# A transformer block's feed-forward stage: two of the seven gate/up products in a stage of their own ahead of the passes, with a second level of seven

## The chip, the core and the metric

The kernel runs on one core of a Trainium2 chip. TensorE (PE) multiplies, VectorE (DVE) and ScalarE (ACT) read its results out of PSUM and prepare operands, GpSimd (POOL) helps with operands in SBUF, and SyncE (SP) issues every DMA, in order. The metric is the device time of one execution in microseconds.

## What is computed

One block of a transformer on 2048 tokens of width 1024, in float32: a modulated layer norm, an attention with a memory over four segments of 512 tokens, a residual, a second modulated layer norm, and a gated feed-forward part with F = 3584 hidden columns:

```
h = layernorm(x) * (1 + ca) + sa
x = x + ga * attention(h)                       # 4 segments of 512 tokens, 32 heads
h = layernorm(x) * (1 + cb) + sb                # h2_d in the kernel, stored transposed: [D, T]
x = x + gb * ((gelu(h @ w_gate) * (h @ w_up)) @ w_down)
```

The change lies in `h @ w_gate` and `h @ w_up`.

## The kernel before

Stages, in the order of TensorE's work: attention; the output projection (`projections`, line 805 on, matmuls of L763), four segments in blocks `block(s, nb)` of 4 tiles; the gate/up stage (`gate_up`, L1188); the down projection (`down`, L1402).

Every float32 product is made of three matmuls of the faster type fp32r: each operand is cut into a high part (ACT, a copy) and a low part (DVE or POOL, the difference), and hi·hi, hi·lo and lo·hi are added up in PSUM. This is what `cut` does (L902 and L904). A matmul here has 128 x 128 weights and 512 columns.

The gate/up stage goes over the tokens in two passes of 1024, and in each pass over the 28 chunks of 128 hidden columns (the second pass backwards): 56 steps, called chunks below, m = 0 to 55. For one chunk, tokens and width are halved, and gate and up are the two column halves. So there are 2 x 2 blocks on each side, a11 to a22 of h2 and b11 = upper gate, b12 = upper up, b21 = lower gate, b22 = lower up, and the four result blocks come from seven products instead of eight (the Winograd form of Strassen's method). Their numbers are those of the code: 1 = a11 b11, 2 = a12 b21, and 3 to 7 are products of sums. The results are gate of the first tokens = 1 + 2; up of the first tokens = 1 + 6 + 5 + 3; gate of the other tokens = 1 + 6 + 7 + 4; up of the other tokens = 1 + 6 + 7 + 5. A product is 4 x 3 = 12 matmuls, so a chunk has 84 and the stage 4704.

The order within a chunk is 1, 6, 2, 7, 5, 4, 3, in three PSUM banks: `pa` takes 1 and then 2 on top of it, `pb` takes 6, then 7 and then 4 on top, `pc` takes 5 and then 3. DVE reads a bank between two products that share it: `u2 = pb + c1` (L1203) after 6, `u3 = pb + c1` (L1213) after 7, `u3 = pc + u3` (L1217) after 5, `g2 = pb + c1` (L1221) after 4, `u2 = pc + u2` (L1226) after 3; then two multiplications in SBUF, `g1 * u2` (L1227) and `g2 * u3` (L1228). ACT copies product 1 to `c1` (L1199) and takes two gelus.

The order on PE, DVE, ACT, POOL and SP is the order in which the program is written. The work beside the products comes from generators in the list `sides`: `step()` is called at fixed places of a product and lets each generator go on by one piece. In the first pass `b_part` loads the weights of a chunk two ahead, forms the sums of `seven` (POOL, L908), cuts them into the tiles B (a ring of 8) and stores all seven to `bc_d`; the second pass reads them back (`b_ahead`). `a_part` and `a_next` make the operands A of h2 for a pass. `w_all` prepares w_down in the second pass (tiles T), and `norm_tiles` makes h2.

Of the kernel before, what the change touches and what calls it, by code (L numbers as in the profile page):

```python
# [36 lines left out]
def block_kernel(ctx: ExitStack, tc: tile.TileContext, x, c, wmod, wq, wkv, wo, beta, wg, wu, wd, out):  # L37
# [11 lines left out]
    mix_d = dram.tile([4 * L, L], F32, name="mix_d")  # L49

    bc_d = dram.tile([FC * 7 * P, 1024], F32, name="bc_d")
# [196 lines left out]
    def norm_tiles(src, dst, segs, jscale, jshift, name, tiles=range(4), wait=0, get=raw_tile, more=[]):  # L248
# [12 lines left out]
        def turn(q, h):  # L261
# [14 lines left out]
            send_h = lambda: nc.sync.dma_start(dv[:, 4 * h:4 * h + 4, tok:tok + P], hh.rearrange("p (k t) -> p k t", t=P))  # L276
# [11 lines left out]
    def norm_steps(toks, xs, load, turn, name, wait):  # L288
        if wait:
            for q in range(len(toks)):  # L290
                load(q)
                for _ in range(wait):
                    yield
                t, nm = xs[q], f"{name}{toks[q]}"
                mv, rs = norm_stats([t[:, :L], t[:, L:]], nm)
                for _ in range(3):
                    yield
                norm_scale([t], mv, rs, nm)
                for _ in range(wait - 2):
                    yield  # L300
                for h in range(2):
                    turn(q, h)
                    yield
            return
        for at in range(5 * len(toks) + 8):
            for q in range(len(toks)):
                k = at - 5 * q
                if k == 0:
                    load(q)
                elif k == 5:  # L310
                    t, nm = xs[q], f"{name}{toks[q]}"
                    st = norm_stats([t[:, :L], t[:, L:]], nm)
                elif k == 7:
                    norm_scale([t], *st, nm)
                elif k in (10, 11):
                    turn(q, k - 10)
            yield
# [409 lines left out]
    xrs = []  # L727
    waiting = [True]

    def x_tile(name):  # L730

        if xrs[0] is None:
            return raw_tile(name)[:, :L]
        xrs[1] += 1
        return f32(xrs[0][:, xrs[1] // 2 % 2, xrs[1] % 2 * L:(xrs[1] % 2 + 1) * L])
# [7 lines left out]
    def project(s, todo):  # L743
# [7 lines left out]
        for n, (i, nb) in enumerate(todo):  # L751
# [16 lines left out]
            store = lambda tok=tok, fs=fs, xr=xr: nc.sync.dma_start(x1_d[tok:tok + P, fs], xr)  # L768
# [43 lines left out]
    def projections():  # L812
# [5 lines left out]
        xrs.extend([wsp_tile("xr"), -1])  # L818
# [17 lines left out]
        sides.append(cols(3))  # L836
        yield from block(2, 0)
        sides.append([ff["b"](0), 2, "b"])
        second = ff["a"]((5, 4))
        operands = ff["a"]((1, 6, 2, 7), second)  # L840
        sides.append([chain(iter([None] * 10), islice(operands, 1)), 1, "n"])
        yield from block(3, 0)
        flush("bn")
        pw_close()
        xrs[0] = None
        ff["pools"](1)
        sides.append([chain(operands, second), 2, "a"])
        yield from block(2, 1)
        pev_close()
        ff["pools"](2)  # L850
        ff["release"]()
        sides.append([chain(iter([None] * 9), islice(ff["b1"], 1)), 1, "a"])
        yield from block(3, 1)

# [3 lines left out]
    PASSES = ((0, 1024), (1024, 1024))  # L858
    NCH = len(PASSES) * FC
# [3 lines left out]
    PRODUCTS = (1, 6, 2, 7, 5, 4, 3)  # L863
# [3 lines left out]
    def feed_forward():  # L867
# [8 lines left out]
        def a_place(i, kt, q):  # L876
            n = 0 if i == 1 else 1 if i in (6, 2) or (i == 7 and kt < 2) else 2 if i in (7, 5) or (i == 4 and kt < 2) else 3
            return ffp[n], f"A{i}_{kt}_{q}"

        def a_tile(i, kt, q, name):  # L880
            at, tag = a_place(i, kt, q)
            return at.tile([P, HM], F32R, name=name, tag=tag, bufs=1)
# [10 lines left out]
        A, B, X, done, loaded, held = {}, {}, {}, set(), [], []  # L893
        ops, raws, cutted = {}, {}, set()

        def parts(n, eng):

            w = 256 if eng is nc.gpsimd else L
            return [slice(k, min(k + w, n)) for k in range(0, n, w)]

        def cut(hi, lo, src, eng):
            nc.scalar.activation(hi, src, AF.Copy)  # L902
            for k in parts(src.shape[-1], eng):
                eng.tensor_sub(lo[:, k], src[:, k], f32(hi)[:, k])  # L904

        def diff(dst, a, b):
            for k in parts(L, nc.gpsimd):
                nc.gpsimd.tensor_sub(dst[:, k], a[:, k], b[:, k])  # L908

        def total(dst, a, b):  # L910
            for k in parts(L, nc.gpsimd):
                nc.gpsimd.tensor_add(dst[:, k], a[:, k], b[:, k])

        def put_a(p, i, kt, src, eng):
            hl = [a_tile(i, kt, q, f"A{p}_{i}_{kt}_{q}") for q in range(2)]
            cut(hl[0], hl[1], src, eng)
            A[p, i, kt] = hl

        def mix_rows(i):
            k = MIX.index(i)  # L920
            return mix_d[k * L:(k + 1) * L]

        def a_mix(p):

            tok, n = PASSES[p]
            h = n // 2
            for kt in range(4):
                r = []
                for k in (kt, kt + 4):
                    t = ra_tile(f"rm{p}_{k}")[:, :n]  # L930
                    nc.sync.dma_start(t, h2_d[k * P:(k + 1) * P, tok:tok + n])
# [4 lines left out]
                s1 = tmp_tile(f"m1_{p}_{kt}")[:, :h]  # L936
                s2 = tmp_tile(f"m2_{p}_{kt}")[:, :h]
                for i, t, f, x, y in ((5, s1, nc.vector.tensor_add, a21, a22), (6, s2, nc.vector.tensor_sub, s1, a11),
                                      (7, a21, nc.vector.tensor_sub, a11, a21), (3, a12, nc.vector.tensor_sub, a12, s2)):
                    f(t, x, y)  # L940
                    later(3, lambda i=i, t=t, kt=kt: nc.sync.dma_start(mix_rows(i)[kt * P:(kt + 1) * P], t))
                    for _ in range(4):
                        yield

        def a_next(p):

            tok, n = PASSES[p]
            h = n // 2
            todo = [(i, b) for i in (1, 6, 2, 7, 5, 4, 3) for b in range(2)]
            rs = []  # L950

            def load():
                q = len(rs)
                if q < len(todo):
                    i, b = todo[q]
                    src = (mix_rows(i) if i in MIX else
                           h2_d[0 if i == 1 else L:L if i == 1 else D, tok + (h if i == 4 else 0):tok + (n if i == 4 else h)])
                    get = ra_tile if q % 3 == 2 else raw_tile
                    t = get(f"ra{p}_{i}_{b}").rearrange("p (k t) -> p k t", k=2)
                    nc.sync.dma_start(t, src[2 * b * P:(2 * b + 2) * P].rearrange("(k p) t -> p k t", p=P))  # L960
# [5 lines left out]
            for q, (i, b) in enumerate(todo):  # L966
                while (p * FC - 1, i) not in done:
# [7 lines left out]
        def a_part(want, following=None):  # L975

            p = 0
            tok, n = PASSES[p]
            h = n // 2

            def put(i, kt, src, eng):

                if len(ffp) > (0, 0, 1, 3, 3 if kt > 1 else 2, 2, 1, 2 if kt > 1 else 1)[i] or len(ffp) == 4:
                    put_a(p, i, kt, src, eng)
                else:
                    held.append(lambda: put_a(p, i, kt, src, nc.vector))

            if want == (5, 4):
                rs = []

                def load(kt):
                    if kt < 4:
                        t = ra_tile(f"rb{p}_{kt}").rearrange("p (k t) -> p k t", k=2)
                        nc.sync.dma_start(t, h2_d.rearrange("(k p) t -> p k t", p=P)[:, kt:kt + 5:4, tok + h:tok + n])
                        rs.append(t)

                load(0)
                load(1)
                yield
                for kt in range(4):  # L1000
                    for _ in range((0, 5, 3, 0)[kt]):
                        yield
                    t = rs[kt]
                    nc.vector.tensor_add(t[:, 0], t[:, 0], t[:, 1])
                    yield
                    put(5, kt, t[:, 0], nc.vector)
                    yield
                    put(4, kt, t[:, 1], nc.vector)
                    yield
                    load(kt + 2)  # L1010
                    yield
                return
            if want == (3,):
                ts = []
                for b in range(2):
                    t = pair_tile(f"r3{p}_{b}", "T", 5)
                    nc.sync.dma_start(t, mix_rows(3)[2 * b * P:(2 * b + 2) * P].rearrange("(k p) t -> p k t", p=P))
                    ts.append(t)
                for _ in range(5):
                    yield  # L1020
                for kt in range(4):
                    put(3, kt, ts[kt // 2][:, kt % 2], nc.vector)
                    yield
                return
            rs = {}

            def load(kt):
                if kt < 4:
                    rs[kt] = []
                    for k in (kt, kt + 4):  # L1030
                        t = (ra_tile, raw_tile)[kt % 2](f"ra{p}_{k}")
                        nc.sync.dma_start(t, h2_d[k * P:(k + 1) * P, tok:tok + n])
                        rs[kt].append(t)

            load(0)
            load(1)
            yield
            for kt in range(4):
                r = rs[kt]
                a11, a21, a12, a22 = r[0][:, :h], r[0][:, h:], r[1][:, :h], r[1][:, h:]  # L1040
# [733 lines left out]
```

## Time and profile before

| | |
|---|---|
| time, median of 3 runs | 2725.58 us (2725.21 to 2725.77) |
| span of the profiled execution | 2724.7 us |
| the profiled execution's own time | its span and what lies around it; against the median that is 0.9 us |
| TensorE busy | 2696.7 us, 99% of the span |
| matmuls of the gate/up stage (L1188) | 4704, from 1111.5 to 2187.7 us |
| DVE, ACT, POOL busy | 1538.4, 1192.3, 851.4 us |
| mean DMA rate | 234 GB/s |

A row of a profile gives an engine's time in a group of instructions, the mean length of one in ns, and how long the engine had been idle before them and what ended that. Matmuls overlap, so the mean length of one (390 ns) is more than the distance between two (busy time divided by count).

### The profile page before, as it was taken

Reading aid. Unit: us, or ns where it says so; the run is one execution under the profiler, and the core shown is the slowest. Engines: PE = TensorE matmul, PEld = TensorE weight load, DVE = VectorE, ACT = ScalarE, POOL = GpSimd, SP = SyncE. Lnnn points to the kernel's source line nnn. Section 1 sums busy time; section 2 is a strip of 40 time slices with the busy share of each in tenths; the row PEclk is TensorE's granted clock in tenths of the full one; section 3 lists DMA queues with packets and bytes.
Section 4 is the critical chain, followed back from the end, with each engine's and each line's share of the span. In section 5 each row is a group of like instructions: output and inputs, shape, how many; then the busy total and the mean of one; then the engine's idle time right before and its main releaser. Section 6 shows DMA issues by size and latency. Waiting matters only on the chain.

```text
span 2724.7 us, 41937 instructions
## 1 busy us (share of the span) xinstructions
PE 2696.7 (99%) x14236; PEld 2251.2 (83%) x14236; DVE 1538.4 (56%) x3447; ACT 1192.3 (44%) x2803; POOL 851.4 (31%) x1446
## 2 busy tenths in 40 slices
PE   7999999999999999999999999999999999999999
PEld 6798888888888788888888888888888888888887
DVE  6676656776777746565555455434343254575456
ACT  6778777776777633334332333111111133233323
POOL 4233334433333534344544451534531000000000
PEclk9999999999999999999999999999999999999999
DMA  7355445435443569788898778999998687795563
GB/s 263 106 157 154 121 128 151 132 113 155 113 125 107 173 222 302 247 307 310 320 359 303 270 274 280 362 361 349 368 354 307 224 315 247 264 304 201 182 209 124
DMA packets 244887, 637.72 MB, mean 234 GB/s; under 512 B 24768, under 2 KB 49344, under 8 KB 244672
## 3 DMA queue, kind: packets, MB, share of 16 engines
q1 hardware_dynamic: 244672, 635.03, 68.1%
q8 instruction: 113, 1.85, 0.3%
q14 instruction: 102, 0.84, 0.1%
HBM read 372.79 MB, written 211.81 MB: 215 GB/s over the span
## 4 chain that ended last, share of the span: by engine, by line
PE 96%; DVE 1%; ACT 1%; DMA 1%; issue 0%; POOL 0%; SPq 0%; ACTq 0%; DVEq 0%; POOLq 0%
PE f L1188 39%; PE y L1402 20%; PE kv L384 9%; PE y L763 6%; PE q L390 6%; PE S L596 3%; PE T L684 3%; PE O L696 3%; PE kT L503 2%; PE vT L503 2%; PE num L652 1%; PE M L635 1%; PE kv L568 1%; ACT sj L600 1%; PE tpb L267 1%; PE kT L418 0%
## 5 line engine op out<-in xcount | busy, mean ns | idle before, releaser
L1188 PE MATMUL f<-A,B 128*128 128x512 f32 x4704 | 1072.3, 390 | 0.0
L1188 PEld LDWEIGHTS f<-A,B 128*128 128x128 f32 x4704 | 881.7, 188 | 183.7 <-issue 1.0
L1402 PE MATMUL y<-B,L 128*128 128x512 f32 x2352 | 533.3, 389 | 0.0
L1402 PEld LDWEIGHTS y<-B,L 128*128 128x128 f32 x2352 | 441.6, 188 | 91.5
L600 ACT ACTIVATE sj<-sj,mm 128x384 f32<-128x384 f32 (+3 forms) x512 | 281.1, 552 | 40.1 <-DVE mm L598 39.6
L598 DVE CUSTOM_DVE_ANT_0 sj<-S,mask 128x384 f32<-128x384 f32 (+3 forms) x512 | 228.2, 488 | 97.6 <-PE S L596 70.8
L687 POOL TENSOR_SCALAR_AFFINE_SELECT pt<-pt 128x128 f32<-128x128 f32 x512 | 166.7, 347 | 331.8 <-ACT pt L686 323.8
L686 ACT ACTIVATE pt<-T 128x256 f32<-128x256 f32 (+3 forms) x512 | 182.3, 444 | 132.5 <-PE T L684 125.8
L902 ACT ACTIVATE L<-X 128x512 fp32r<-128x512 f32 x168 | 105.8, 630 | 259.3 <-PE y L1402 169.1
L904 DVE TENSOR_TENSOR L<-X,L 128x512 fp32r<-128x512 f32 x168 | 115.9, 691 | 147.4 <-ACT L L902 143.3
L1222 ACT ACTIVATE g<-g 128x512 f32<-128x512 f32 x56 | 35.4, 632 | 370.7 <-DVE g L1221 370.7
L375 POOL TENSOR_TENSOR w<-r,w 128x256 fp32r<-128x256 f32 x180 | 133.7, 773 | 141.4 <-ACT w L369 136.5
L384 PE MATMUL kv<-w,hha 128*128 128x256 f32 x896 | 173.8, 284 | 2.3 <-DVE vx L402 2.3
L1127 POOL TENSOR_TENSOR rw<-rw,gbb 128x256 f32<-128x256 f32 x112 | 90.7, 845 | 249.2 <-DMA rw<-wd 167.7
L384 PEld LDWEIGHTS kv<-w,hha 128*128 128x128 f32 x896 | 143.9, 191 | 3.4 <-DVE vx L402 2.5
L763 PE MATMUL y<-wo,hho 128*128 128x512 f32 x384 | 126.7, 395 | 0.0
L384 PE MATMUL kv<-w,hla 128*128 128x256 f32 x448 | 126.6, 283 | 0.0
L1209 ACT ACTIVATE g<-f 128x512 f32<-128x512 f32 x56 | 33.5, 598 | 207.8 <-PE f L1188 207.8
L1199 ACT ACTIVATE c<-f 128x512 f32<-128x512 f32 x56 | 33.4, 597 | 173.9 <-PE f L1188 173.9
L684 PE MATMUL T<-qs,ks 128*128 128x256 f32 (+3 forms) x512 | 105.6, 327 | 1.8 <-DVE ry L663 1.1
L596 PE MATMUL S<-ks,qs 96*128 96x384 f32 (+3 forms) x512 | 106.9, 329 | 0.2
L684 PEld LDWEIGHTS T<-qs,ks 128*128 128x128 f32 x512 | 80.9, 189 | 25.0 <-issue 12.1
(255 smaller groups left out, 4275.1 us busy)
## 6 DMA issues: line engine op xcount, KB each, us to landing
bc_d<-B SPq DMA_DIRECT2D x189, 512.0 KB, 5.0
B<-bc_d SPq DMA_DIRECT2D x189, 512.0 KB, 5.5
B<-wc_d SPq DMA_DIRECT2D x112, 512.0 KB, 4.2
hid_d<-g SPq DMA_DIRECT2D x56, 512.0 KB, 4.3
wc_d<-T SPq DMA_DIRECT2D x56, 512.0 KB, 7.1
X<-hid_d SPq DMA_DIRECT2D x112, 256.0 KB, 4.6
wr<-gd_d SPq DMA_DIRECT2D x84, 256.0 KB, 4.0
qs<-qh SPq DMA_DIRECT2D x64, 256.0 KB, 3.5
```

The source lines that it names most:

```text
L375: nc.gpsimd.tensor_sub(w[:, 1, c], r[:, c], f32(w[:, 0, c]))
L384: nc.tensor.matmul(ps, b[:, sl], w[:, a], start=(kt == 0 and a == 0 and b is hi), stop=(kt == KT - 1 and a == 1), **kw)
L390: nc.tensor.matmul(ps, w[:, a], b, start=(kt == 0 and a == 0 and b is hi), stop=(kt == KT - 1 and a == 1), **kw)
L596: nc.tensor.matmul(ps[:, :nk], qs[:96, j, i * P:(i + 1) * P], ks[:96, j, :nk], start=True, stop=True)
L598: nc.vector.tensor_tensor_reduce(out=sj[:, :nv], in0=ps[:, :nv], in1=mask[:, L - nv:], scale=-1.0, scalar=3.4e38, op0=ALU.add, op1=ALU.min ...
L600: nc.scalar.activation(sj[:, :nv], sj[:, :nv], AF.Exp, bias=mm[:, j, i:i + 1], scale=-1.0, accum_out=ll[:, i, j:j + 1])
L684: nc.tensor.matmul(ps[:, :nn], ks[:, j, kc * P:(kc + 1) * P], qs[:, j, L - nn:], start=True, stop=True)
L686: nc.scalar.activation(pt, ps[:, nn - n:nn], AF.Exp)
L687: nc.gpsimd.affine_select(pt[:, :P], pt[:, :P], pattern=[[1, P]], compare_op=ALU.is_ge, fill=0.0, base=0, channel_multiplier=-1)
L763: nc.tensor.matmul(ps, b[:, i * P:(i + 1) * P], w[:, a, g % 2], start=(g == 0 and a == 0 and b is hi), stop=(g == G - 1 and a == 1))
L1188: nc.tensor.matmul(ps, B[m, i][:, a, kt * P:(kt + 1) * P], A[p, i, kt][b], start=(start and kt == 0 and a == 0 and b == 0), stop=(kt == 3 ...
L1402: nc.tensor.matmul(banks[t], ops[k][:, y, t * P:(t + 1) * P], B[slots[k]][:, x], start=(i not in (2, 4, 3) and j == 0 and x == 0 and y == ...
```

## The change

Products 1 and 2 leave the chunks. A new stage ahead of the passes makes them for all 2048 tokens, two chunks at a time (n = 0 to 13, called double chunks below). In it each of the two is again a 2 x 2 block product: the token halves are the two passes' first 512 tokens, the width is halved again, and the two column halves are the gate columns of chunks 2n and 2n+1. Each is done by seven products of a second level, in the same numbering. A product of the second level is 2 x 3 = 6 matmuls, so a double chunk has 2 x 7 x 6 = 84 matmuls where its two chunks in two passes had 4 x 24 = 96.

Results of the stage go to `st_d`: c1 (product 1) and g1 (the gelu of 1 + 2). `cg_load` reads them one chunk ahead of use. A chunk has the five products 6, 7, 5, 4, 3, in the banks `pb`, `pb`, `pc`, `pb`, `pc`. The ring of 8 tiles B now holds five per chunk; of the five the first pass stores 6 and 7 whole, 5 and 4 as uncut sums (`bt_d`), and 3 not at all; the second pass cuts 5, 4 and 3 again (`b_again`). A chunk calls `step()` 10 times. The new stage uses the mm banks of the projection for `pa` and the s banks for `pb` and `pc`.

To have h2 of the first halves of both passes when the stage begins, the projection makes block (2,1) before (2,0), the norm of segment 2 runs beside block (3,0) and that of segment 3 inside the new stage; `a_early` and `a_first` make the stage's 28 operand pairs AA, `a_next(0)` makes the first pass's operands beside the last double chunk.

```
@@ gate_up @@
-            pa, pb, pc = (s_ps(f"f{q}_{m}") for q in range(3))
-            c1, u2, u3 = (c_tile(f"c{q}_{m}") for q in range(3))
-            product(pa, 1, True)
-            nc.scalar.activation(c1, pa, AF.Copy)
+            c1, g1 = cg.pop(m)
+            pb, pc = (s_ps(f"f{q}_{m}") for q in range(2))
+            u2, u3 = (c_tile(f"c{q}_{m}") for q in range(2))
             product(pb, 6, True)
             nc.vector.tensor_add(u2, pb, c1)
-            product(pa, 2, False)
-            g1, g2 = (g[:, q] for q in range(2))
-            nc.scalar.activation(g1, pa, AF.Gelu_apprx_tanh)
+            step()
             product(pb, 7, False)
             nc.vector.tensor_add(u3, pb, c1)
...
+        def two(n):
+            def product(i, r):
+                while ("a", i, r, 1) not in A:
+                    next(ff["first"])
+                if r == 1:
+                    pa[i] = mm_ps(f"pa{n}_{i}")
+                elif r == 6:
+                    pb[i] = s_ps(f"pb{n}_{i}")
+                elif r == 5:
+                    pc[i] = s_ps(f"pc{n}_{i}")
+                ps = (pa if r < 3 else pb if r in (6, 7, 4) else pc)[i]
+                w = B["a", n, r]
+                for k in range(2):
+                    at = (i - 1) * 2 * P + k * P
+                    for a, b in ((0, 0), (0, 1), (1, 0)):
+                        nc.tensor.matmul(ps, w[:, a, at:at + P], A["a", i, r, k][b], ...)
+            def ended(i, r):
+                if r == 1:
+                    nc.scalar.activation(c[i], pa[i], AF.Copy)
+                    return
+                if r in (6, 7, 4):
+                    nc.vector.tensor_add(t, pb[i], c[i])
+                elif r in (5, 3):
+                    nc.vector.tensor_add(t, pc[i], t)
+                elif i == 1:
+                    nc.scalar.activation(t, pa[i], AF.Copy)
+                else:
+                    nc.vector.tensor_add(t, pa[i], out[1][q][:, p])
...
+                if r != 2:
+                    total(t, t, out[1][q][:, p])
+                later(2, lambda: nc.scalar.activation(t, t, AF.Gelu_apprx_tanh))
+                later(4, put)
+            for i, r in [(i, r) for i in (1, 2) for r in ROUND] if n == 0 else [(i, r) for r in ROUND for i in (1, 2)]:
+                product(i, r)
+                ended(i, r)
+                step()
...
+        def b_again(q):
...
+            for k in range(0, q + 3):
+                e = right[k]
+                if again.get(e) is not None:
+                    t = B[e]
+                    cut(t[:, 0], t[:, 1], again[e], nc.vector)
+                    again[e] = None
```

Three places of the order. In its rows, a semaphore named in brackets is the engine or DMA queue whose work the instruction waits for.

TensorE in a chunk of the first pass before: the end of product 6, all of whose matmuls write the bank `pb` (here f_10_16444), then product 2 in `pa` (f_10_16443), then product 7 in `pb` again:

```order
L1188 MATMUL f_10_16444<-A_6_3_1_14519,B_6_16359 128x512
L1188 MATMUL f_10_16444<-A_6_3_0_14518,B_6_16359 128x512
L1188 MATMUL f_10_16443<-A_2_0_0_14357,B_2_16371 128x512 [waits Activation_49]
L1188 MATMUL f_10_16443<-A_2_0_1_14358,B_2_16371 128x512
...
L1188 MATMUL f_10_16443<-A_2_3_0_14522,B_2_16371 128x512
L1188 MATMUL f_10_16444<-A_7_0_0_14371,B_7_16392 128x512 [waits DVE_49]
L1188 MATMUL f_10_16444<-A_7_0_1_14372,B_7_16392 128x512
```

The same place now:

```order
L1325 MATMUL f_5_18038<-A_6_3_1_17237,B_6_17954 128x512
L1325 MATMUL f_5_18038<-A_6_3_0_17236,B_6_17954 128x512
L1325 MATMUL f_5_18038<-A_7_0_0_17252,B_7_17972 128x512 [waits DVE_49,Activation_49]
L1325 MATMUL f_5_18038<-A_7_0_1_17253,B_7_17972 128x512
L1325 MATMUL f_5_18038<-A_7_0_0_17252,B_7_17972 128x512
```

The first matmul of product 7 waits for DVE's read of the bank, as it did; the 12 matmuls of product 2 that stood between are gone.

DVE from one chunk of the second pass to the next, before (L1226 is the add after product 3, L1227 and L1228 the two multiplications, L1203 the next chunk's add after product 6):

```order
L1221 TENSOR_TENSOR g_19579<-f_30_19519,c_30_19521 128x512 [waits DMAHW0_49,PE_49]
L1226 TENSOR_TENSOR c_30_19522<-f_30_19520,c_30_19522 128x512 [waits PE_49]
L1227 TENSOR_TENSOR g_19579<-g_19579,c_30_19522 128x512 [waits DVE_49]
L1228 TENSOR_TENSOR g_19579<-g_19579,c_30_19523 128x512 [waits Activation_49]
L1203 TENSOR_TENSOR c_31_19664<-f_31_19661,c_31_19663 128x512 [waits PE_49,Activation_49]
```

The same place now (L1350, L1351, L1352 and L1335 are those four; in every other chunk or so a cut of a tile T stands behind that of B_5):

```order
L1346 TENSOR_TENSOR g_22470<-f_42_22378,cg_0_22256 128x512 [waits DMAHW0_49,PE_49]
L922 TENSOR_TENSOR T_7_22481<-rw_0_22240,T_7_22481 128x512 [waits DMAHW7_49,DMAHW4_49,Activation_49]
L1350 TENSOR_TENSOR c_42_22380<-f_42_22379,c_42_22380 128x512 [waits PE_49]
L1351 TENSOR_TENSOR g_22470<-cg_1_22257,c_42_22380 128x512 [waits DMAHW2_49,DVE_49]
L1352 TENSOR_TENSOR g_22470<-g_22470,c_42_22381 128x512
L922 TENSOR_TENSOR B_5_22382<-ag_5_22405,B_5_22382 128x512 [waits DMAHW7_49,Activation_49]
L922 TENSOR_TENSOR T_5_22511<-rt_22391,T_5_22511 128x512 [waits Activation_49]
L1335 TENSOR_TENSOR c_43_22499<-f_43_22497,cg_0_22374 128x512 [waits DMAHW5_49,PE_49]
```

Between one product 3 and the next product 6 stood two products' worth of matmuls (1 and 6) before, and stands one now; a cut or two has come ahead of the add.

DVE at the end of the last projection block, now (y_1_2 and y_1_3 are the last two tiles, L777 their read-out; u are h2's blocks read back, s and the AA_6 to AA_3 the new stage's sums and cuts):

```order
L777 TENSOR_TENSOR xr_14531<-y_1_1_14602,xr_14531 128x512 [waits PE_49]
L1018 TENSOR_TENSOR s_1_0_14663<-u_0_1_14645 128x512 [waits DMAHW6_49,DMAHW4_49,Activation_49]
L1020 TENSOR_TENSOR u_0_0_14643<-s_1_0_14663,u_0_0_14643 128x512 [waits DMAHW1_49,DVE_49,Pool_49]
L922 TENSOR_TENSOR AA_6_0_1_14677<-u_0_0_14643,AA_6_0_0_14676 128x512 [waits Activation_49]
L1018 TENSOR_TENSOR s_1_1_14680<-u_1_1_14649 128x512 [waits DMAHW7_49,DMAHW6_49]
L1020 TENSOR_TENSOR u_1_0_14647<-s_1_1_14680,u_1_0_14647 128x512 [waits DMAHW5_49,DVE_49,Pool_49]
L922 TENSOR_TENSOR AA_6_1_1_14692<-u_1_0_14647,AA_6_1_0_14691 128x512 [waits Activation_49]
L922 TENSOR_TENSOR AA_7_0_1_14696<-u_0_1_14645,AA_7_0_0_14695 128x512 [waits Activation_49]
L922 TENSOR_TENSOR AA_7_1_1_14706<-u_1_1_14649,AA_7_1_0_14705 128x512 [waits Activation_49]
L922 TENSOR_TENSOR AA_5_0_1_14710<-s_1_0_14663,AA_5_0_0_14709 128x512 [waits Activation_49]
L777 TENSOR_TENSOR xr_14531<-y_1_2_14669,xr_14531 128x512 [waits DMAHW1_49,PE_49]
```

The read-out of tile y_1_2, whose mm bank the new stage's first product takes over, stands behind nine instructions on h2's last segment; before, the first chunk's banks were others (s), and no mm bank was needed after the projection until the down stage.

576 lines of the change are left out of this document (326 added, 250 removed).

## The prediction

> **What bounds the kernel now.** I read the page first, then TensorE's waits, the stages, and one chunk in order of time.
>
> ```profile
> span 2724.7 us, 41937 instructions
> PE 2696.7 (99%) x14236; PEld 2251.2 (83%) x14236; DVE 1538.4 (56%) x3447; ACT 1192.3 (44%) x2803; POOL 851.4 (31%) x1446
> PEclk9999999999999999999999999999999999999999
> PE 96%; DVE 1%; ACT 1%; DMA 1%; issue 0%; POOL 0%; SPq 0%; ACTq 0%; DVEq 0%; POOLq 0%
> L1188 PE MATMUL f<-A,B 128*128 128x512 f32 x4704 | 1072.3, 390 | 0.0
> ```
>
> TensorE works 99% of the span at the full clock, and the chain of waits is TensorE for 96%. The gate/up line never waits: idle 0.0. A matmul costs 1072.3/4704 = 0.228 us there, and each one taken away is worth that, as long as the wait stays at zero.
>
> ```profile
> PE scp L143 <- DVE scdg L137: 11.1, 1, 11.1
> PE kv L384 <- DVE vx L402: 2.3, 1, 2.3
> PE T L684 <- DVE qs L620: 0.4, 2, 0.3
> ...
> 960.00:1111.50 151.50, 151.50 (x702) 125.26 (x702) 79.50 (x149) 51.20 (x91) 51.47 (x64) 1.00 0.79 259
> 1111.50:1650.00 538.50, 538.50 (x2404) 445.16 (x2403) 295.43 (x441) 188.85 (x340) 257.39 (x332) 1.00 0.81 300
> 1650.00:2187.70 537.70, 537.70 (x2373) 445.09 (x2372) 200.47 (x271) 88.50 (x156) 172.26 (x224) 1.00 0.89 327
> ```
>
> Those are TensorE's waits (all in the attention and its opening) and three stretches of time: projection, first and second pass (PE, PEld, DVE, ACT, POOL busy, clock, DMA share, GB/s). TensorE fills each stretch wholly; DVE has slack on average, 295 of 538 us at most. What counts is therefore whether one wait appears in a place that is passed often.
>
> **The change, part by part.**
>
> *Matmuls removed.* 56 chunks x 24 = 1344 become 14 x 84 = 1176. 168 x 0.228 = **-38.3 us**. Sizes stay. DMA falls (the second pass reads two whole tiles per chunk, not seven); nothing waits for it now, so that is worth 0.
>
> *Product 7 right behind product 6.* Both write `pb`, and DVE's add of `pb` must end in between. Till now 12 matmuls in another bank covered it; now nothing does, in each of 56 chunks. Behind the waiting matmul queues all that TensorE has left to do, since its order is fixed. The price is a round trip TensorE, DVE, TensorE, which these rows in order of time (start, length) give piece by piece:
>
> ```profile
> 1570.59 0.62 PE L1188 MATMUL f<-A,B 128*128 128x512 f32 x2
> ...
> 1571.02 0.69 DVE L1217 TENSOR_TENSOR c<-f,c 128x512 f32<-128x512 f32 x1 [1.01 <-PE f L1188]
> ...
> 1661.74 0.68 DVE L1203 TENSOR_TENSOR c<-f,c 128x512 f32<-128x512 f32 x1
> 1662.47 1.69 PEld L1188 LDWEIGHTS f<-A,B 128*128 128x128 f32 x8 [0.39 <-DVE c L1203]
> ...
> 82.79 0.39 PE L384 MATMUL kv<-w,hha 128*128 128x256 f32 x1 [2.25 <-DVE vx L402]
> ...
> 83.01 0.28 PE L384 MATMUL kv<-w,hla 128*128 128x256 f32 x1
> ...
> 83.13 0.40 PE L384 MATMUL kv<-w,hha 128*128 128x256 f32 x2
> ```
>
> The first of the two matmuls at 1570.59 ends a product (1570.59 + 0.39 = 1570.98; the second starts 0.23 later, too late to end before the add), and the add that waits for it starts at 1571.02: 0.43 from start to start. The add takes 0.69. The one weight load that waited for such an add starts 0.05 after its end (1661.74 + 0.68 = 1662.42, then 1662.47). So the next matmul starts 1.17 after the last, not 0.228: 0.94 lost. After a wait the array also starts slowly: 82.79 to 83.01 is 0.22, the next distance 0.12, so 0.10 more. 1.04 x 56 = **+58.2** (52.6 without the slow start, 63.8 if that costs twice as much).
>
> *The add comes late.* It stands in DVE's queue behind the end of the chunk before; first four rows in order of time, then groups (busy, mean ns of one), then a late multiplication:
>
> ```profile
> 1576.46 0.69 DVE L1226 TENSOR_TENSOR c<-f,c 128x512 f32<-128x512 f32 x1 [2.03 <-PE f L1188]
> 1577.18 0.69 DVE L1227 TENSOR_TENSOR g<-g,c 128x512 f32<-128x512 f32 x1
> 1577.79 0.69 DVE L1228 TENSOR_TENSOR g<-g,c 128x512 f32<-128x512 f32 x1
> 1578.39 0.68 DVE L904 TENSOR_TENSOR B<-t,B 128x512 fp32r<-128x512 f32 x1
> ...
> L1203 DVE TENSOR_TENSOR c<-f,c 128x512 f32<-128x512 f32 x56 | 38.7, 691 | 101.4 <-PE f L1188 98.4 <-ACT B L902 2.8
> L1227 DVE TENSOR_TENSOR g<-g,c 128x512 f32<-128x512 f32 x56 | 49.0, 874 | 2.8
> L1228 DVE TENSOR_TENSOR g<-g,c 128x512 f32<-128x512 f32 x56 | 45.8, 818 | 0.0
> L904 DVE TENSOR_TENSOR T<-t,T 128x512 fp32r<-128x512 f32 x14 | 14.1, 1006 | 2.4 <-ACT T L902 2.4
> ...
> 1826.74 2.37 DVE L1227 TENSOR_TENSOR g<-g,c 128x512 f32<-128x512 f32 x1
> 1829.03 0.68 DVE L1228 TENSOR_TENSOR g<-g,c 128x512 f32<-128x512 f32 x1
> ```
>
> From the add after product 3 DVE is free 1.93 later (1576.46 to 1578.39), 0.61 an instruction. Product 6 takes 12 x 0.228 = 2.74, so the first pass has 0.8 to spare. In the second pass the cut of B_5 takes 0.61 of it (0.2 left), and in 11 of 27 chunks a cut of T another 0.61 (0.4 late). Instructions with both inputs in SBUF also stretch: 0.87 and 0.82 on average for the multiplications, where 0.69 is undisturbed, once 2.37; together 0.3 a chunk. Adds out of PSUM don't (0.691). The cut of T stretches by 0.3 (1006 against 691), and I allow 0.2 for that of B_5, so that the 11 are 0.4 + 0.3 + 0.3 + 0.2 = 1.2 late and the 16 others some 0.2: 11 x 1.2 + 16 x 0.2 = **+16** (5 without any stretch, 27 with about twice as much).
>
> [...]
>
> *The new stage's beginning.* The first double chunk needs h2 of segment 2, normed only beside the last two projection blocks, and 24 of its 28 operand pairs are cut from then on. The nearest view is the same place before, DVE's rows in order of time, TensorE's first chunk, and the medians from a DMA's issue to its landing:
>
> ```profile
> 1104.13 0.68 DVE L767 TENSOR_TENSOR xr<-y,xr 128x512 f32<-128x512 f32 x1
> 1110.22 0.69 DVE L1004 TENSOR_TENSOR rb<-rb 128x512 f32<-128x512 f32 x1 [2.94 <-DMA rb<-h_d]
> 1112.23 1.28 DVE L767 TENSOR_TENSOR xr<-y,xr 128x512 f32<-128x512 f32 x2
> ...
> 1111.71 1.07 PE L1188 MATMUL f<-A,B 128*128 128x512 f32 x4
> ...
> x_d<-xr SPq DMA_DIRECT2D x32, 256.0 KB, 4.0
> h_d<-htb SPq DMA_DIRECT2D x32, 256.0 KB, 4.4
> ra<-h_d SPq DMA_DIRECT2D x14, 512.0 KB, 5.9
> ```
>
> There DVE waited for h2 to come back, and the read-out of a tile that ended near 1106 was made at 1112.23. It cost nothing, for the chunk that began at 1111.71 used other banks. Now the first product wants that bank. By the DMA rows the chain store of x1, store of h2, load (4.0 + 4.4 + 5.9 = 14.3) ends about 1 us before the projection does, since SP's queue holds the store of h2 back until that of x1 has landed. From there to the last add of the double chunk stand 52 DVE instructions (32 us at 0.61), and four of its sums go to POOL and ACT and back (2 us each): 40 us where TensorE has 19. **+20** (6 if the data come early and nothing waits, 32 if POOL stretches the cuts).
>
> *The last double chunk* has 34 DVE instructions (11 adds, 20 cuts of A, 3 of B, 21 us) behind five loads that land 6 to 7 us into it, for 19 us of matmuls: +6 (0 to 12). *Double chunks 1 to 12*: about 18 DVE instructions each, but the first waits for weights loaded at the chunk's own start, which leaves the adds of 6 and 7 just in time: +3 (0 to 12). *Change of pass*: four cuts of A ahead of the add, 2.44 - 0.8, and some drift: +2.5 (1 to 5). The stage's work on ACT and POOL lies beside matmuls:
>
> ```profile
> L902 ACT ACTIVATE A<-ra 128x512 fp32r<-128x512 f32 x40 | 22.4, 621 | 7.9 <-DMA ra<-h_d 7.0 <-DMA ra<-mix_d 0.7
> L908 POOL TENSOR_TENSOR ru<-ru 128x256 f32<-128x256 f32 x56 | 41.1, 755 | 0.0
> ```
>
> A double chunk has 14 instructions of each kind, 8.7 us on ACT and 10.6 on POOL under 19 us of matmuls. Without that cover, as at the stage's two ends, it is part of the chains counted there. New on SP's queue are 8 stores to `st_d` in a double chunk and 2 loads in a chunk, read a chunk ahead of use; the queue loses more than that (7 stores and 7 loads of B a chunk become 4 and 5), so I cost it at nothing. If a load of c1 came late, the add of `pb` would, and each microsecond would be TensorE's.
>
> Sum: -38.3 + 58.2 + 16 + 20 + 6 + 3 + 2.5 = +67. The profiled span is 2724.7 and the median 2725.58, 0.9 around it: **2793 us**. With all low ends it is +26 (2752), with all high ends +114 (2839).
>
> **Rivals.**
>
> *No wait (faster).* If product 7 could start while `pb` is still read, or its wait were covered, both chunk terms vanish: -38.3 + 31.5 = -7, 2719. It decides from 0.12 us a chunk down. For it: 4704 matmuls with idle 0.0 today. Against it: the wait is in the order, and its shortest part, the add, is 0.69. Chance 4%; another 3% for no change, with most terms at or below their ends.
>
> *The new stage starts clean.* If h2 comes back early and the cuts keep up, the 29 us at its ends go and only the chunks' waits remain: 2764. For it: DVE is 55% busy. Against it: the rows at 1110. Chance 20%.
>
> *DVE becomes the bound in the second pass.* If the 2.37 us stretch is the rule, since POOL's work on w_down is squeezed into fewer microseconds, every chunk there loses 1.5 more: 27 x 1.5 = 40, 2833. Chance 13%.
>
> *The clock.* Rows with waits kept it:
>
> ```profile
> 70.00:100.00 30.00, 25.93 (x177) 21.31 (x177) 19.46 (x58) 21.44 (x58) 10.76 (x24) 1.00 0.38 97
> ```
>
> 4 us idle of 30 left it at 1.00. Were every chunk's wait followed by 3 us at half speed, it would add 56 x 1.5 = 84: 2877. [...] Chance 3%.
>
> **How the numbers follow.** The forecast itself has 57%. 0.2% (5 us) is about what a measurement of this kernel tells from no change. Faster 4%, same 3%, slower 93%. The range takes in the clean start and the DVE-bound case at their likelier ends: 2752 to 2835.
>
> **What would show it.** After: the line of the chunks' matmuls has 3360, with about 75 us idle before them, ended by the add after product 6, near 1.0 us each in the first pass and more in the second; the stage's 1176 matmuls have 20 to 30 us, most in the first double chunk, the first of it ended by a read-out of the projection. Wrong if the idle time at product 7 is under 0.7 us a chunk, if the stage starts without a wait, or if the clock falls.

## The result, and the profile after

| | before | after |
|---|---|---|
| time, median | 2725.68 us | 2897.61 us (4 runs, 2895.0 to 2905.21) |
| ratio, with its 95% interval | | 1.0636 [1.0619, 1.0652] |
| span of the profiled execution | 2724.7 us | 2893.3 us |
| gate/up work: before, the chunks; after, the new stage + the chunks | 1076.2 us | 333.8 + 906.1 us |

The change makes the kernel 6.4% slower. The forecast was 2793 us, with a range up to 2835: the direction is right, the size is less than half of what came.

First the page of the changed kernel (span, TensorE, its clock, the chain that ended last, and the matmuls of the chunks and of one bank of the new stage), then TensorE's waits (us in total, times, longest):

```profile
span 2893.3 us, 42626 instructions
PE 2716.8 (94%) x14068; PEld 2233.6 (77%) x14068; DVE 1766.4 (61%) x3746; ACT 1260.1 (44%) x2924; POOL 1056.1 (37%) x1646
PEclk9999999999999998999999999989999999999999
PE 73%; DVE 10%; DMA 8%; issue 4%; POOL 3%; ACT 2%; SPq 1%; DVEq 0%; POOLq 0%; ACTq 0%
L1325 PE MATMUL f<-A,B 128*128 128x512 f32 x3360 | 802.3, 399 | 103.4 <-DVE c L1335 93.2
L1106 PE MATMUL pb<-AA,BB 128*128 128x512 f32 x504 | 132.3, 411 | 29.8 <-DVE x L1122 21.9
...
PE f L1325 <- DVE c L1335: 93.2, 56, 7.0
PE pb L1106 <- DVE x L1122: 21.9, 13, 5.8
PE pa L1106 <- ACT c L1116: 9.3, 8, 2.7
PE f L1325 <- DVE c L1341: 9.1, 4, 2.8
PE pb L1106 <- DVE y L1122: 7.8, 3, 5.2
PE pa L1106 <- DVE xr L777: 6.2, 1, 6.2
```

L1335 is the add after product 6. TensorE waits for it 56 times, once in every chunk, as forecast, but 93.2 us in all and not 75. The chain of waits, 96% TensorE before, is TensorE for 73% now. The clock has two slices under 9. By stage (PE, PEld, DVE, ACT, POOL busy, clock, DMA share, GB/s):

```profile
1116.40:1450.20 333.80, 292.41 (x1208) 230.03 (x1209) 216.20 (x339) 139.45 (x247) 172.47 (x211) 0.94 0.55 185
1450.20:2356.30 906.10, 802.74 (x3365) 642.15 (x3365) 510.42 (x655) 200.86 (x359) 470.94 (x552) 0.97 0.79 281
```

At 0.228 us a matmul the chunks would take 3360 x 0.228 = 766 and the stage 1176 x 0.228 = 268. They take **140** and **66** more. Idle time explains 103.4 of the 140. In the stage it is 333.8 - 292.4 = 41 (47 with the 6.2 ahead of its first matmul). By the trace's record of the granted clock TensorE worked for 45.9 us of the chunks and for 27.3 of the stage at half of the full clock, and half of that time is lost: 23 and 14. So about 37 us of the loss are clock, a term that the forecast's sum did not have. Some 14 and 11 us are left; in the chunks that is about what 56 waits cost beyond their idle time (1.10 - 0.81 each, as e2_before_adjacent shows below).

What stands ahead of the add differs by place. A chunk of the first pass whose add is not late, then one of the second (start, length, idle before and what ended it; rows of other work between these are left out):

```profile
1666.72 0.69 DVE L1350 TENSOR_TENSOR c<-f,c 128x512 f32<-128x512 f32 x1
1667.45 1.02 DVE L1351 TENSOR_TENSOR g<-cg,c 128x512 f32<-128x512 f32 x1
1667.87 2.32 POOL L922 TENSOR_TENSOR t<-ru,rg 128x256 f32<-128x256 f32 x2
1668.38 1.22 DVE L1352 TENSOR_TENSOR g<-g,c 128x512 f32<-128x512 f32 x1
1669.53 0.68 DVE L1335 TENSOR_TENSOR c<-f,cg 128x512 f32<-128x512 f32 x1
1670.35 5.95 PE L1325 MATMUL f<-A,B 128*128 128x512 f32 x25 [0.95 <-DVE c L1335]
...
2033.10 0.68 DVE L1350 TENSOR_TENSOR c<-f,c 128x512 f32<-128x512 f32 x1
2033.81 1.21 DVE L1351 TENSOR_TENSOR g<-cg,c 128x512 f32<-128x512 f32 x1
2034.43 2.31 POOL L922 TENSOR_TENSOR rt<-rw,rt 128x256 f32<-128x256 f32 x2
2034.94 1.23 DVE L1352 TENSOR_TENSOR g<-g,c 128x512 f32<-128x512 f32 x1
2036.09 1.21 DVE L922 TENSOR_TENSOR B<-ag,B 128x512 fp32r<-128x512 f32 x1
2037.21 1.20 DVE L922 TENSOR_TENSOR T<-t,T 128x512 fp32r<-128x512 f32 x1
2038.34 0.68 DVE L1335 TENSOR_TENSOR c<-f,cg 128x512 f32<-128x512 f32 x1
2039.08 7.10 PE L1325 MATMUL f<-A,B 128*128 128x512 f32 x30 [3.44 <-DVE c L1335]
```

In the first case two multiplications stand there, stretched to 1.02 and 1.22 beside GpSimd's work (the POOL row) where 0.69 is undisturbed, and TensorE still waits only 0.95. In the second there are also the cuts of B_5 and of T, and all four take 1.20 to 1.23 beside GpSimd's work on w_down. TensorE waits 3.44, 2.6 more than the 0.81 of a bare wait (e2_before_adjacent).

### The profile page after: what moved, and what is told of

Its sections match the earlier page's. It is cut to its first block, busy times and chain, and to the rows that moved or that the text cites. A ratio compares the mean times of both kernels' runs of the same rounds, so it can differ in the third digit from the quotient of the medians.

```text
span 2893.3 us, 42626 instructions
## 1 busy us (share of the span) xinstructions
PE 2716.8 (94%) x14068; PEld 2233.6 (77%) x14068; DVE 1766.4 (61%) x3746; ACT 1260.1 (44%) x2924; POOL 1056.1 (37%) x1646
## 3 DMA queue, kind: packets, MB, share of 16 engines
q8 instruction: 111, 1.82, 0.3%
## 4 chain that ended last, share of the span: by engine, by line
PE 73%; DVE 10%; DMA 8%; issue 4%; POOL 3%; ACT 2%; SPq 1%; DVEq 0%; POOLq 0%; ACTq 0%
PE y L1525 18%; PE f L1325 18%; PE kv L395 8%; PE q L401 6%; PE y L773 5%; PE S L607 3%; PE T L695 3%; PE O L707 3%; DMA g<-wg 2%; DVE BB L922 2%; PE kT L514 2%; PE vT L514 1%; DVE g L1352 1%; DVE c L1335 1%; PE pb L1106 1%
## 5 line engine op out<-in xcount | busy, mean ns | idle before, releaser
L1325 PE MATMUL f<-A,B 128*128 128x512 f32 x3360 | 802.3, 399 | 103.4 <-DVE c L1335 93.2
L1325 PEld LDWEIGHTS f<-A,B 128*128 128x128 f32 x3360 | 641.5, 192 | 263.8 <-DVE c L1335 63.9
L1239 POOL TENSOR_TENSOR rw<-rw,gbb 128x256 f32<-128x256 f32 x112 | 103.2, 957 | 221.2 <-DMA rw<-wd 207.2
L1106 PE MATMUL pb<-AA,BB 128*128 128x512 f32 x504 | 132.3, 411 | 29.8 <-DVE x L1122 21.9
L1106 PEld LDWEIGHTS pb<-AA,BB 128*128 128x128 f32 x504 | 97.3, 197 | 57.4 <-DVE x L1122 27.9
L925 ACT ACTIVATE B<-t 128x512 fp32r<-128x512 f32 x84 | 52.2, 621 | 147.6 <-POOL t L922 147.6
```

The costliest lines, as they stand in the source:

```text
L1106: nc.tensor.matmul(ps, w[:, a, at:at + P], A["a", i, r, k][b], start=(r in (1, 6, 5) and k == a == b == 0), stop=(k == 1 and a == 1), skip ...
L1325: nc.tensor.matmul(ps, B[m, i][:, a, kt * P:(kt + 1) * P], A[p, i, kt][b], start=(start and kt == 0 and a == 0 and b == 0), stop=(kt == 3 ...
```

## The experiments

Theory A: the wait behind product 6 costs a bare round trip of some 1.1 us; what stands ahead of the add in VectorE's queue makes it longer; the longer waits pull the clock down; and the new stage loses time to adds that stand behind cuts. Theory B: the second pass is bound by VectorE or by transfers, and the wait only shows where that ends.

### The wait taken away: products in the order 6, 5, 7, 3, 4

```
-    PRODUCTS = (6, 7, 5, 4, 3)
+    PRODUCTS = (6, 5, 7, 3, 4)
...
             nc.vector.tensor_add(u2, pb, c1)
             step()
+            product(pc, 5, True)
+            nc.vector.tensor_add(u3, pc, c1)
+            step()
             product(pb, 7, False)
-            nc.vector.tensor_add(u3, pb, c1)
+            nc.vector.tensor_add(u3, pb, u3)
             step()
-            product(pc, 5, True)
-            nc.vector.tensor_add(u3, pc, u3)
+            product(pc, 3, False)
...
```

> The changed kernel with the five products of a chunk in the order 6, 5, 7, 3, 4, so that no bank is used twice in a row; the new stage and all work counts are as they were. Theory A (the waits behind product 6 are the whole loss of the chunks: the round trip, what stands ahead of the add in VectorE's queue, and a clock that falls after the longer of these waits): the chunk stage goes from 906 us to 770 to 790 (3360 x 0.228 = 766 and the start of chunk 0), so 2763 to 2783 in all, idle before the chunks' matmuls under 15 us, clock above 0.99. Theory B (the second pass is bound by VectorE or by transfers, and the wait only shows where it ends): only the 56 round trips of 1.0 to 1.2 go, 2830 to 2842, and new idle time appears behind another product.

Measured: 2783.89 us, ratio 1.0209 [1.0192, 1.0226]; the chunks took 789.5 us, the stage 333.9 as in the changed kernel. TensorE's waits in the chunks, and VectorE's longest wait for a load there:

```profile
PE f L1330 <- DVE c L1346: 7.1, 3, 3.4
PE f L1330 <- DVE c L1340: 6.7, 3, 5.8
PE f L1330 <- ACT B L925: 4.9, 2, 3.2
...
DVE m L959 <- DMA rm<-h_d: 13.9, 4, 4.5
```

The 56 waits are gone and 117 of the 140 us with them; the time is 0.9 us above theory A's band (18.7 us of idle were left, where under 15 was expected). Theory B falls: VectorE's and the DMA queue's work is the same, and TensorE is not held by it. What is left is chunk 0, and four sums (`m<-rm`) for the second pass whose loads came too late.

### The wait alone, in the kernel before

Product 7 is put ahead of product 2 in 52 chunks:

```
+        def order(m):
+            return PRODUCTS if m in (0, FC - 1, FC, NCH - 1) else (1, 6, 7, 2, 5, 4, 3)
...
+            for i in order(m)[2:4]:
```

> The kernel before, with products 2 and 7 exchanged in 52 of its 56 chunks, so that 7 follows 6 in the same bank; nothing else of the change. Product 1 stands between the chunk's end and product 6, so the add after 6 is not late. The prediction's price of the bare round trip, 1.04 each: 52 x 1.04 = 54, 2780 us. The undisturbed chunks of the changed kernel, 14.83 against 13.62 us: 52 x 1.21 = 63, 2789 us. Rival (each wait, however short, pulls the clock down for a product): 52 x 2.5 or more = 130, 2856 us, clock under 0.99.

Measured: 2782.79 us, ratio 1.0208 [1.0193, 1.0223].

```profile
PEclk9999999999999999999999999999999999999999
PE f L1196 <- DVE c L1211: 42.9, 53, 0.9
```

52 waits (the row has one more, of 0.3, at the change of pass) cost 2782.8 - 2725.5 = 57.3 us, 1.10 each (1.01 to 1.17 by the interval), 0.81 of it idle. The prediction's 1.04 stands. No wait there was longer than 0.9, and the clock kept every slice at 9: waits of that length did nothing to it.

### The add first in VectorE's queue

```
-                    b_again(q)
+                    if i != 6:
+                        b_again(q)
...
-                    if kt == 1:
+                    if kt == 1 and i != 6:
                         step()
...
             nc.vector.tensor_add(u2, pb, c1)
+            if p > 0:
+                b_again((m - FC - 1) * 5)
+            step()
```

> The changed kernel with the order of products kept, but the cut of the operand two products ahead and the side step within product 6 issued behind the add of product 6, so that only the two multiplications of the chunk before stand ahead of that add in VectorE's queue. Theory A (lateness in the queue makes the long waits, and the long waits make the slow clock): every chunk costs 1.2 us over 13.62, the chunk stage goes from 906 to 845 to 860 us, 2837 to 2852 in all, longest wait behind product 6 under 2 us outside chunk 0, clock at 0.99 or more. Rival (the stretched multiplications make the add late, or the clock falls after any wait): less than 20 us are won, 2878 or more, and waits over 2 us stay in the second pass.

Measured: 2855.35 us, ratio 1.0485 [1.0467, 1.0502]; chunks 863.1 us at a clock of 0.99, 3 us over the expected band.

```profile
PE f L1326 <- DVE c L1336: 62.3, 56, 8.6
PE f L1326 <- DVE c L1345: 9.9, 4, 2.7
...
2021.41 1.22 DVE L1356 TENSOR_TENSOR g<-g,c 128x512 f32<-128x512 f32 x1
2022.55 0.68 DVE L1336 TENSOR_TENSOR c<-f,cg 128x512 f32<-128x512 f32 x1
2023.28 7.09 PE L1326 MATMUL f<-A,B 128*128 128x512 f32 x30 [1.29 <-DVE c L1336]
```

This is the same chunk of the second pass as above: the multiplications are as stretched as before, but the two cuts now come behind the add, and the wait is 1.29, not 3.44. So lateness in the queue, with the clock that follows it, was 906.1 - 863.1 = 43 us. Of that 103.4 - 72.8 = 31 are idle time; half-clock work costs 10 us of the chunks here, 23 in the changed kernel. One wait of over 2 us behind product 6 is left outside chunk 0, where none was expected: 3.45 us at the change of pass, where cuts of A stand ahead of the add too.

### A dose of waiting

On the kernel with the wait alone, with `dose` 1 to 6 in 17 chunks and 0 in the others:

```
...
+            for _ in range(dose):
+                nc.vector.tensor_add(u3, pb, c1)
             nc.vector.tensor_add(u2, pb, c1)
```

> The kernel of the run before (52 bare waits, 1.10 us each), with 1 to 6 more adds of the same bank issued on VectorE ahead of the add after product 6, in 17 of the 56 chunks, a chunk without them after each; they are 57 in all, results unchanged. Their waits are to be about 0.8 + 0.61 for each more, so 1.4 to 4.5 us. Theory A (a wait costs its length up to some 2 us; from there on the clock falls and product 7, 12 matmuls, takes 1.5 to 2.5 us longer than 2.74): the chunks with 1 more lose only the 0.61, those with 3 and more lose 1.5 to 2.5 us besides, and the run takes 2782 + 35 + 20 to 30 = 2837 to 2847 us. Rival (what was slow behind long waits in the changed kernel was operands that came late, not the clock): product 7 keeps 2.74 us after every wait, 2817 us.

Measured, in a single run: 2844.41 us, in theory A's band. Two stretches behind a wait, the first of 1.45 us, the second of 2.83:

```profile
1786.20:1789.20 3.00, 2.96 (x13) 2.46 (x14) 0.00 (x0) 0.00 (x0) 0.00 (x0) 1.00 0.93 339
1871.80:1874.80 3.00, 2.98 (x10) 2.41 (x11) 0.00 (x0) 0.00 (x0) 3.00 (x5) 0.75 1.01 384
```

Thirteen matmuls against ten, at a clock of 1.00 and 0.75. From the end of one wait to the start of the next TensorE takes 19.33 us in a chunk without more adds (from chunk 14 on; in the first chunks other delays lie over it). Over that, behind waits of

| 1.45, 1.54, 2.27 | 2.11, 2.83, 3.00, 3.63, 3.72 and 4.28 | 4.44 and 5.01 |
|---|---|---|
| 0.0 us | 1.6 to 1.7 | 2.4 to 2.7 |

So it is the clock, not a late operand, and it comes as a step. That 2.27 costs nothing (the 6 us behind it ran at 1.00) and 2.11 does (0.72) is taken up in the last section.

### The new stage: adds ahead of cuts, loads two ahead

```
                     load(2, 1)
+                    yield from wait_for(8)
...
-                    diff(a21, a11, a21)
+                    diff(a21, a11, a21, nc.vector if i == 2 else nc.gpsimd)
...
-            if 0 < n < NJ - 1:
-                b_two_load(n + 1) if n + 1 not in two_raws else None
+            for k in (n + 1, n + 2):
+                if n > 0 and k < NJ and k not in two_raws:
+                    b_two_load(k)
```

> The changed kernel with three edits in the new stage: the operands of the second pair of tokens in the first double chunk are cut eight steps later, so that the adds of the products stand ahead of them in VectorE's queue; their differences run on VectorE and not on GpSimd; the gate weights of a double chunk are loaded two ahead and not one. Theory A (the stage's 66 us over 1176 x 0.228 are adds that stand behind cuts that wait for loads): 12 to 30 us are won, 2868 to 2886. Rival (VectorE's and ScalarE's own work in the first double chunk bounds it, and the late normed tokens): under 6 us, 2892 to 2898, the waits only change their place.

Measured: 2879.8 us, ratio 1.0563 [1.0547, 1.0579]; 17.8 us won. The stage itself went from 333.8 to 309.4; the chunks took 912.2 and lost 6 again, of which chunk 0's wait of 9.2 us, not 7.0, is 2. TensorE's two waits for adds of `pb` (x and y) after the first 30 us of the stage:

```profile
PE pb L1107 <- DVE y L1123: 4.3, 3, 2.8
PE pb L1107 <- DVE x L1123: 2.9, 3, 1.5
```

All but two of these, 0.19 and 0.32, lie in the last double chunk: double chunks 1 to 12 run clean once their weights are loaded two ahead. What stays is the first double chunk, 44 us in both kernels, and the last. The loads won most of it: 22 us lie in double chunks 1 to 12, while the other two edits bear on the first.

### Three attempts to take out the rest

The first has the order of e1_alternate, the stage edits, and four more, shown here: later sums for the second pass, an earlier load for chunk 0, later cuts of the second double chunk's weights, and later cuts of A. The second and third change other things for chunk 0 on top of it.

```
-                for _ in range(4):
+                for _ in range(4 if p == 0 else 8):
...
+                if (n, i, r) == (NJ - 1, 2, 4):
+                    cg_load(0)
...
+                sides.append([chain(islice(ahead, 1), wait_for(5), ahead) if n == 0 else ahead, 1, "b"])
...
-            yield
+            yield from wait_for(7 if p == 0 else 1)
```

> The changed kernel with the order 6, 5, 7, 3, 4 of e1_alternate, the stage edits of e4_stage, and four more: the sums of the second pass's operands wait eight steps, not four, for their loads; the load of c1 and g1 for chunk 0 is issued before the last double chunk's last products, not after them; the cuts of the second double chunk's weights start five steps later; the cuts of A for the first pass start seven steps behind their loads, not one. Theory A (waits at named places are the whole difference to 268 us of matmuls in the stage and 766 in the chunks): the stage takes 280 to 300 and the chunks 770 to 782, so 2725.5 - 1076 + 6 + 1050 to 1082 = 2706 to 2738 us. Rival (VectorE's work in the first and last double chunk and the late normed tokens set their length, so stalls only change place): stage 305 to 335, 2745 us or more.

> The kernel of e6_combined with four edits at its last stalls: c1 and g1 of chunk 0 go to tiles that are free earlier and are loaded at the start of the last double chunk, as are the weights of chunk 1; the first product of the stage uses a bank that the projection does not; the sums of both operands of the first double chunk's second pair are made one behind the other before either is cut. In e6_combined chunk 0 waited 10.2 us for c1 and 4.8 for its weights and ran slow behind both, some 20 us; the stage began 5.4 us late. Theory A (each named wait goes and nothing takes its place): chunks 766 to 772, stage 285 to 298, 2746 - 17 - 3 to 10 = 2718 to 2728 us, at or a little under the kernel before. Rival (the loads of A and of chunk 0 share one queue and stall each other, so the end of the stage grows by what chunk 0 wins): 2738 us or more.

> The kernel of e6_combined with two edits: c1 and g1 of chunk 0 are loaded at the start of the last double chunk into tiles free by then (as in e7_combined2, whose other edits are left out), and seven, not five, of the ten operand loads for the first pass are issued there, the two more into tiles for weights that stand empty. In e7_combined2 chunk 0 still waited 7.0 us, now behind cuts of A whose loads the DMA queue held back for a free tile. Theory A (that queue is what holds the end of the stage and chunk 0): the wait at chunk 0 falls under 2 us, the stage's end wins some 5, chunks 766 to 774, in all 2718 to 2732 us. Rival (VectorE's own 21 us of adds and cuts in the last double chunk hold it): 2736 us or more, and chunk 0 waits as before.

Measured: 2746.22 us, ratio 1.0076 [1.0063, 1.009]; 2742.96, 1.0058 [1.0044, 1.0072]; 2747.07, 1.0084 [1.007, 1.0098]. Theory A's bands were missed all three times, by 8, 15 and 15 us; each total lay in its rival's band. TensorE's waits in the chunks, one kernel after the other:

```profile
PE f L1333 <- DVE c L1343: 10.5, 2, 10.2
PE f L1333 <- ACT B L925: 6.5, 2, 4.8
```

```profile
PE f L1332 <- DVE c L1342: 9.1, 3, 7.0
...
1397.12 0.95 SPq L1194 DMA_DIRECT2D cg<-st_d  x2
...
1437.76 0.69 DVE L922 TENSOR_TENSOR A<-ra,A 128x512 fp32r<-128x512 f32 x1 [2.36 <-ACT A L925]
...
1439.57 0.68 DVE L1342 TENSOR_TENSOR c<-f,cg 128x512 f32<-128x512 f32 x1
```

```profile
PE f L1331 <- ACT B L925: 10.6, 2, 7.5
PE f L1331 <- DVE c L1341: 7.5, 3, 5.5
```

I had put chunk 0's wait down to c1's load. In the second kernel that load was issued 42 us ahead of the add, and the add still came 7.0 us late, now behind cuts of A. In the third more of A's loads were early, and the weights of chunk 0's fourth product came late (7.5, at the 37th matmul of the chunks). The rivals were right that stalls change their place here. The bare total fell a long way, though: these kernels are 5.2 to 5.3% faster than the changed one, and 0.6 to 0.8% slower than the one before. None beats both, so none is proposed.

## Why the prediction was right or wrong

The terms of its sum beside what the runs show:

| term | predicted | measured |
|---|---|---|
| 168 matmuls less | -38.3 | not measured alone; the chunks without waits take 0.228 a matmul |
| product 7 right behind 6 | +58.2 (52.6 to 63.8) | 56 x 1.10 = 61.7 |
| the add late, change of pass | +18.5 | 43: 31 idle, the rest mostly clock (e3_add_first, where the change of pass keeps its wait) |
| the rest of the chunks | 0 | 863.1 - 766 - 61.7 = 35 |
| the new stage, with its start | +29 | 66 + 6 = 72 |

The last column, with the matmuls at their forecast, adds up to 173, or 168 after the 4 us by which the kernel before was itself over 0.228 a matmul, and some 1 us in earlier stages; the spans differ by 168.6. The fourth row is what is left of the 140, so the sum alone confirms no row.

*Right:* the bare wait, its place, its releaser and its price; that it is passed 56 times; that the stage's first wait is a read-out of the projection (6.2 us); and that the sum is a loss, since the matmuls saved are worth 38.

*Wrong, the add that comes late.* The step that failed is the stretch: "together 0.3 a chunk", from the means 0.87 and 0.82 of 56 multiplications. The count was right: a cut of T stands ahead of the add in 12 of the 27 chunks, where 11 were forecast. But the means mixed 0.69 with 1.2. In the late chunk above GpSimd works beside all four instructions ahead of the add, they lose 0.5 each at once, and a lateness of 1.2 us became 2.6; in eleven of the 12 TensorE waits 2.8 to 3.6, in the other 1.2. The add itself, out of PSUM, stayed at 0.68 in both chunks shown. The overlap does not always stretch: of 211 VectorE instructions of the changed kernel with two inputs in SBUF that lay nine tenths or more beside GpSimd's work from 1120 to 2340 us, 109 took 1.15 to 1.3, and 32 stayed at 0.67 to 0.72. The rival "DVE becomes the bound" had the stretched rows and, with 40 us, nearly the 43, but that is luck: it had 1.5 us in every chunk of the second pass, while 12 of the 28 wait 0.78, no more than a bare wait.

*Wrong, the clock.* It was not in the sum at all. As a rival it had about the right price, 1.5 us, against the 1.6 to 1.7 of the dose; but its 3 us at half speed were an assumption that no row stood for, and it was set as all 56 waits or none, at 3%. The row that spoke against it, 4 us idle of 30 at 1.00, held one wait of 2.25 us and none longer, and that it kept the clock was luck. The same 30 us of the attention in the profile of the changed kernel, with a wait of 2.3:

```profile
70.00:100.00 30.00, 27.12 (x183) 23.27 (x181) 19.47 (x62) 21.37 (x60) 14.14 (x30) 0.94 0.40 107
```

So nearly the same wait went with 1.00 in one profile and with 0.94 in the other. Waits of up to 0.9 left the clock alone, 53 times in e2_before_adjacent. The term belonged to the long waits alone: 23 us in the chunks and 14 in the stage.

*Wrong, the stage*, the largest miss: 72 us for 29. Against 84 x 0.228 a double chunk, the first one with its start lost 31 us (forecast 20), double chunks 1 to 12 together 28 (forecast 3), the last 12 (forecast 6). "About 18 DVE instructions each ... +3" saw that the first cut waits for its load, and took the adds of 6 and 7 for just in time behind it; they were late, and loading two ahead won 22 us there in e4_stage. The first and the last double chunk were priced for idle time and not for the clock that falls there (all of the stage's half clock lies from 1116 to 1157 and from 1429 to 1450 us). What sets the length of the first is not settled: e4_stage left it at 44 us, and e6_combined took some 10 off it and added 7 to the second.

*Not seen at all:* the sums `m<-rm` of the second pass, in chunks 1, 3, 5 and 7, stand in VectorE's queue until their loads land; and chunk 0. In e3_add_first these four chunks take 18.02, 19.27, 19.28 and 18.83 us from add to add where the others take 14.83, 16 us in all. Of the other 19 in that row some 5 lie at the change of pass and 2 in chunk 24; most of the rest is chunk 0.

The range reached to the dearest single rival. What came is several at once: a late add means a long wait, and a long wait can mean a slow clock; the stage's late loads come on top. They should have been added up, not set side by side.

## What to carry to other kernels

Price a new wait first by its bare round trip, then by what stands ahead of the releasing instruction in its engine's queue at that place, stretched as it is stretched there and not on average. If that brings an idle time past about 2 us (2.11 in the dose), count the slow matmuls behind it too, 1.7 us here; one profile in which such a wait kept the clock does not rule them out. Two products into one bank, one right behind the other, are cheap to avoid by another order of the same products: here that gave back 117 of 140 us.

## What the runs showed of the hardware

The same length of wait does not always pull the clock down. Two waits of the changed kernel, of 3.44 and of 3.23 us, with the 6 us behind each:

```profile
2039.08:2045.08 6.00, 6.00 (x26) 4.98 (x27) 2.06 (x4) 0.00 (x0) 1.83 (x2) 1.00 0.97 308
2299.23:2305.23 6.00, 6.00 (x19) 4.80 (x20) 3.05 (x4) 0.00 (x0) 5.73 (x7) 0.72 0.96 305
```

Of its 17 waits over 2.1 us behind product 6 ten were followed by a clock of 0.72 or less over 6 us, seven by 1.00; of the shorter ones none. In the trace's record of its granted clock, every stretch at half clock in the stage and the chunks starts on one grid of 3.413 us, within 0.01, and is one, two or three steps of it long. Those steps around the first of the two waits, then around the second:

```profile
2033.83:2037.24 3.41, 1.80 (x8) 1.15 (x7) 3.41 (x4) 0.36 (x1) 3.41 (x4) 1.00 0.76 305
2037.24:2040.65 3.41, 1.57 (x7) 1.31 (x8) 2.38 (x4) 0.00 (x0) 3.41 (x4) 1.00 0.92 298
2040.65:2044.06 3.41, 3.41 (x17) 2.83 (x16) 1.29 (x2) 0.00 (x0) 0.26 (x1) 1.00 0.98 323
...
2296.65:2300.07 3.42, 0.84 (x4) 0.70 (x5) 3.42 (x5) 0.00 (x0) 3.42 (x4) 1.00 0.93 319
2300.07:2303.48 3.41, 3.41 (x10) 2.63 (x9) 0.85 (x1) 0.00 (x0) 3.41 (x5) 0.50 0.97 282
```

The first wait leaves 1.61 and 1.84 us idle in two steps, and the clock stays; the second leaves 2.58 in one, and the next step runs at half. Of the 264 steps that lie wholly in this kernel's chunks 249 ran at full clock: the 237 with at most 1.93 us idle were followed by full clock, the 12 with 2.06 or more by half clock. So what went with the clock there is the idle time within one step, and a wait's length only together with its place. In the dose the 6 us behind the waits fit a grid of the same step, to 0.04; on it the wait of 2.27 is split into 1.0 and 1.3, and that of 2.11 lies in one step. In the changed kernel's chunks a half clock stayed after steps with 0.76 us idle or more and ended after those with 0.00. Behind the dose's waits of 4.44 and 5.01 the 6 us ran at 0.51 and 0.57, which is 5.9 and 5.2 us at half clock and so more than one step. One step at half clock costs 3.41 / 2 = 1.7, as the 1.6 to 1.7 measured. In the stage these numbers are not the whole account: there the clock also fell after a step with 1.82 us idle. Of single waits 2.11 us was enough once, and 3.44 was not.
